# RWKV-7 scan and SwiGLU block in one kernel: gate and value matmuls all in half-height tiles, outputs in bursts on shared PSUM pairs

## The chip, the cores and the metric

The kernel runs on one core of a Trainium2 chip. A core has five engines that run their own instruction lists and wait for each other through semaphores: TensorE (PE, matmuls and transposes, with its weight loads shown apart as PEld), VectorE (DVE), ScalarE (ACT), GpSimd (POOL) and SyncE (SP), and beside them the DMA queues. PE writes its results to PSUM, here used as pairs of banks of 128 partitions x 2 x 512 numbers; DVE and ACT read them from there. Everything is computed in 32-bit floats.

The metric is the device time of one execution in microseconds. The profile is that of one execution; its span runs from the first to the last instruction.

## What is computed

A recurrent attention block (4 batches x 8 heads, 768 steps, head size 40) is followed by a gated feed-forward block on its output (3072 tokens x 320, inner size 1536). Cut to what matters:

```python
for t in range(S):                                   # S = 768
    y[:, :, t] = einsum('bhd,bhde->bhe', r_t, state)
    Sa = einsum('bhde,bhe->bhd', state, a_t)
    state = state * w_t[:, :, None, :] - einsum('bhd,bhe->bhde', Sa, b_t) \
            + einsum('bhd,bhe->bhde', v_t, k_t)
x = y.transpose(0, 2, 1, 3).reshape(B * S, H * D)    # 3072 x 320
xn = x / sqrt(mean(x * x, -1) + 1e-6) * rms_g
g, val = xn @ w_gate, xn @ w_val                     # 320 -> 1536, twice
out = (g * sigmoid(g) * val) @ w_out                 # 1536 -> 320
```

The three weight matrices arrive as 64-bit floats and are made into 32-bit ones on the chip.

## The kernel before

**The scan.** The 768 steps are cut into 24 chunks of 32 steps; one chunk of all batches is 128 tokens. For a chunk, `front(c)` loads r, k, v, w, a, b, turns them by PE transposes and builds products of decays over levels 1, 2, 4, 8, 16 and 32 (`gramk` matmuls on PE, many multiplications on DVE and copies on ACT). `inverse(c)` solves a small triangular system per head on DVE, with DMAs through DRAM before and after it. `main(c)` advances the state (`state`, `lower`, `update`), computes the outputs of the chunk (`score`, `level`, `y0`), turns them back (`turn4`), normalizes each token (ACT's square and scale, a power on POOL) and turns the result once more (`turn3`) into `xg`, the feed-forward's input with features on the partitions. The 320 features lie in `xg` as two blocks of 128 and one of 64, the last one twice, on the upper and on the lower 64 partitions. `front` and `inverse` of chunk c + 2 are created after `main(c)`.

**The feed-forward.** Chunks are gathered into groups by `GROUPS`: one chunk, eleven times two, one. After the last chunk of a group, `feed(g)` goes over the 1536 inner features in 12 slices of 128 (index `f`), two slices to a PSUM pair, a "room" (`plan.room()`). Gate lies in the first bank of the pair and value in the second. For a slice PE does the last 64 features first, gate on the upper 64 rows of the array beside value on the lower 64 (`h64`), then the two blocks of 128 features at full height, gate and then value (`hh`). ACT takes silu of the gate into `sg`, DVE multiplies value by it into `hT`, and PE multiplies `hT` by the slice's output weights (`out`) and adds that up over all 12 slices in `po`, a pair of its own that nothing else uses. After slice 12 ACT copies `po` to `o` and four DMAs write it out. Every matmul of 32-bit floats is two weight loads and two matmul instructions in the profile.

**The weights.** `narrow_slice(f)` loads the slices of the three weight matrices as raw 64-bit words and narrows them in two halves; each half is four DVE instructions and three of ACT, 24 halves in all. The slices are laid side by side in `wf[f]`. This is done during the first group; slices 2 to 11 are loaded through POOL's queue.

**The order.** Every step above is a "piece" for one engine (`plan.add`; `pe` puts several matmuls in one piece). All pieces are created first, with the pieces that each needs, and then issued in one order for all engines, written out by hand as 5993 numbers (`ORDER`): each is the place of a piece, counted from the first one not yet issued. An engine runs its pieces strictly in that order. The digits of `PAIRS` give each room one of three PSUM pairs; a pair is held from a room's first piece to its last. `plan.issue` also tells the framework where two instructions on one pair touch different banks or partition quarters and need not wait for each other.

All PE matmuls are issued through line 532 and transposes through line 535, DVE's instructions through line 486 (the narrowing's last one through 1050), ACT's through 509, 513, 516 and 1046, and DMAs through 529, so that the profile's rows are told apart by tiles: `ps<-xg,wf` is gate and value, `po<-wf,hT` the output.

Of the kernel before, what the change touches and what calls it, by code (L numbers as in the profile page):

```python
# [7 lines left out]
FP32 = mybir.dt.float32  # L8
I32 = mybir.dt.int32
# [11 lines left out]
GROUPS = (1,) + (2,) * 11 + (1,)  # L21
# [3 lines left out]
WARM = 230.0  # L25
# [380 lines left out]
def kernel(  # L406
# [587 lines left out]
    def feed(g):  # L994
# [5 lines left out]
        for f in range(LEAD if g == 0 else 0):  # L1000
            narrow_slice(f)
# [110 lines left out]
```

## Time and profile before

| what | before |
|---|---|
| runs, us | 1020.66, 1022.94, 1028.27 (median 1022.94) |
| span of the profiled execution, us | 1017.9 |
| median of the runs less that span, us | 5.0 |
| PE busy | 928.0 us, 91% |
| DVE busy | 779.5 us, 77% |
| ACT busy | 510.6 us, 50% |
| POOL busy | 343.2 us, 34% |
| mean granted TensorE clock | 0.953 of full |

How it is read: busy time is the union of an engine's instructions, and it is an average over stages; the page's slices show which engine is full when. A matmul's length in the profile holds the time until its result is out, so in a stream the distance between two starts is shorter than the length. The profile does not give the profiled execution's own time apart from its span; the median of the runs stands 5.0 us above it.

### The profile page before, as it was taken

The page shows a single profiled execution, that of the slowest core. Times are in us where ns is not written, and L with a number is a line of the kernel's source. Part 1 is how long each engine was busy: PE and PEld are TensorE (multiplying, and loading weights), DVE is VectorE, ACT ScalarE, POOL GpSimd, SP SyncE. Part 2 cuts the span into 40 slices and gives each one's busy share as a digit, 9 for nine tenths or more (in the row PEclk, how much of TensorE's full clock was granted, in tenths as well). Part 3 has the DMA queues.
Part 4 walks back from the last instruction along what each step waited for, and adds up shares of the span by engine and source line. Part 5 has one row for each costly group of instructions (what it writes and reads, how often), then busy time and mean ns, then how long its engine had stood idle before and what let it go on. Part 6 is the DMA issues. An engine that isn't in the chain of part 4 may idle for free.

```text
span 1017.9 us, 55372 instructions
## 1 busy us (share of the span) xinstructions
PE 928.0 (91%) x24512; PEld 754.3 (74%) x24512; DVE 779.5 (77%) x2718; ACT 510.6 (50%) x1134; POOL 343.2 (34%) x595
## 2 busy tenths in 40 slices
PE   3457779998999999999999999999999999999998
PEld 3446668877777777787877778777787787787776
DVE  9989987786967976967868779669688788776531
ACT  6878656544454544454463444544535545435131
POOL 9966543313233233224321433224233323400000
PEclk9657768999999999999999999999999999999999
DMA  7764543313333223233231242232322422420100
GB/s 170 159 178 109 124 91 78 74 32 69 52 67 63 51 60 75 43 67 68 48 75 32 61 88 48 50 70 45 70 58 46 78 48 60 76 45 9 45 6 20
DMA packets 140175, 68.87 MB, mean 68 GB/s; under 512 B 120768, under 2 KB 127264, under 8 KB 139936
## 3 DMA queue, kind: packets, MB, share of 16 engines
q0 software_dynamic: 19680, 32.48, 15.8%
q1 hardware_dynamic: 118080, 32.54, 15.2%
q8 instruction: 192, 3.15, 1.3%
q10 hardware_dynamic: 2176, 0.33, 0.2%
q14 instruction: 47, 0.39, 0.1%
HBM read 55.05 MB, written 10.22 MB: 64 GB/s over the span
## 4 chain that ended last, share of the span: by engine, by line
PE 71%; DVE 12%; issue 5%; DMA 5%; ACT 3%; SPq 3%; DVEq 0%; ACTq 0%
PE ps L532 50%; PE po L532 14%; PE ps L535 6%; SPq L529 3%; DVE Yi L486 3%; DMA sY<-Yi 2%; DVE tmp L486 2%; DVE As L486 1%; DVE y L486 1%; ACT VU L513 1%; DVE LT L486 1%; DMA sB<-LT 1%; DVE K L486 1%; DVE wf L486 1%; DMA LT<-sY 1%
## 5 line engine op out<-in xcount | busy, mean ns | idle before, releaser
L532 PE MATMUL ps<-xg,wf 128*128 128x256 f32 (+3 forms) x1872 | 360.5, 374 | 2.4 <-issue 1.6
L532 PEld LDWEIGHTS ps<-xg,wf 128*128 128x128 f32 (+1 forms) x1872 | 267.5, 189 | 50.6 <-issue 14.5
L532 PE MATMUL po<-wf,hT 128*128 128x320 f32 x576 | 180.5, 447 | 0.5 <-issue 0.5
L486 DVE TENSOR_TENSOR hT<-ps,sg 128x256 f32<-128x256 f32 (+1 forms) x156 | 59.9, 399 | 95.3 <-PE ps L532 53.7
L532 PEld LDWEIGHTS po<-wf,hT 128*128 128x128 f32 x576 | 102.6, 189 | 37.8 <-issue 3.7
L486 DVE TENSOR_TENSOR tmp<-Yi,M 128x24 f32<-128x24 f32 (+21 forms) x512 | 107.3, 210 | 12.2 <-DMA M<-sB 1.4
L486 DVE TENSOR_TENSOR Yi<-Yi,tmp 128x24 f32<-128x24 f32 (+21 forms) x512 | 107.1, 209 | 11.1
L509 ACT ACTIVATE sg<-ps 128x256 f32<-128x256 f32 (+1 forms) x156 | 54.1, 368 | 116.9 <-PE ps L532 114.1
L529 POOL DMA_DIRECT2D VU<-in_v_dram x92 | 54.1, 590 | 145.7 <-PE ps L532 145.6
L486 DVE TENSOR_TENSOR K<-K,T 128x256 f32<-128x256 f32 (+1 forms) x191 | 91.9, 496 | 2.1 <-ACT T L513 0.7
L529 POOL DMA_DIRECT2D kbn<-in_k_dram x92 | 53.9, 588 | 101.3 <-PE ps L532 98.3
L519 POOL TENSOR_TENSOR ss<-ss,mhalf 128x1 f32<-128x1 f32 x24 | 14.4, 599 | 214.7 <-DVE ss L486 214.6
L532 PE MATMUL ps<-Ab,K 64*60 64x56 f32 (+2 forms) x4608 | 77.9, 223 | 7.3 <-issue 2.2
L532 PEld LDWEIGHTS ps<-Ab,K 64*60 64x60 f32 (+2 forms) x4608 | 71.2, 135 | 17.0 <-issue 10.3
L513 ACT COPY KN<-ps 128x640 f32<-128x640 f32 x95 | 65.1, 691 | 33.4 <-DVE LT L486 22.4
L529 POOL DMA_DIRECT2D kbn<-in_b_dram x92 | 54.1, 589 | 77.5 <-PE ps L532 76.3
L486 DVE TENSOR_TENSOR As<-ps,msi 128x256 f32<-128x256 f32 (+1 forms) x168 | 70.5, 455 | 10.6 <-PE ps L532 6.4
L532 PEld LDWEIGHTS ps<-As,KN 128*40 128x40 f32 x3072 | 67.2, 128 | 12.9 <-issue 7.4
L532 PE MATMUL ps<-As,KN 128*40 128x32 f32 x3072 | 72.1, 208 | 4.2 <-issue 2.7
L513 ACT COPY K<-K 128x512 f32<-128x512 f32 x95 | 60.3, 635 | 23.5 <-PE ps L532 12.0
L486 DVE SCALAR_TENSOR_TENSOR Yi<-M,Yi 128x31 f32<-128x31 f32 (+6 forms) x228 | 44.7, 244 | 33.5 <-DMA M<-sB 17.1
L529 POOL DMA_DIRECT2D wn<-in_w_dram x92 | 52.1, 568 | 19.6 <-DVE KN L486 18.5
(138 smaller groups left out, 1525.4 us busy)
## 6 DMA issues: line engine op xcount, KB each, us to landing
M<-sB SPq DMA_DIRECT2D x96, 128.0 KB, 3.0
wan<-in_r_dram SPq DMA_DIRECT2D x24, 160.0 KB, 4.0
kbn<-in_b_dram POOLq DMA_DIRECT2D x92, 40.0 KB, 2.6
kbn<-in_k_dram POOLq DMA_DIRECT2D x92, 40.0 KB, 2.8
VU<-in_v_dram POOLq DMA_DIRECT2D x92, 40.0 KB, 2.8
wan<-in_a_dram POOLq DMA_DIRECT2D x46, 80.0 KB, 2.9
wan<-in_w_dram POOLq DMA_DIRECT2D x46, 80.0 KB, 3.0
wn<-in_w_dram POOLq DMA_DIRECT2D x92, 40.0 KB, 2.5
```

Source lines behind the costliest of these rows:

```text
L486: plan.add("DVE", time + more + each * size(o), 0.087, lambda at: [fn(at(o), *m(at))], [o], aps(*args))
L509: scalar(o, [a], lambda at: nc.scalar.activation(at(o), at(a), f, **kw), aps(acc), 0.1 if f in (AF.Square, AF.Relu) else 0.0)
L513: scalar(o, [a], lambda at: nc.scalar.copy(at(o), at(a)), extra=more)
L519: plan.add("POOL", 0.5, 0.06, lambda at: nc.gpsimd.tensor_tensor(o, a, b, op), [o], [a, b])
L529: plan.add(by, 0.6 if by == "POOL" else 0.45, 0.0, lambda at: queue.dma_start(out=o, in_=i), [o], [i], load=load, since=since)
L532: return o, lhsT, rhs, lambda at: nc.tensor.matmul(at(o), lhsT, rhs, start=start, stop=stop, skip_group_check=True), 4
L535: return o, i, ident, lambda at: nc.tensor.transpose(at(o), i, ident), 2
```

## The change

- Gate and value: the 320 features lie in `xg` as five blocks of 64, each twice, on the upper and the lower 64 partitions. All matmuls of gate use the upper 64 rows of the array, all of value the lower 64, five of each for a slice, issued in turn (two pieces: blocks 0 to 2, blocks 3 and 4). The weights are laid out for that, with three DMAs for each half of a slice (before two and four).
- To get `xg` in that form the normalized chunk is copied with each 64 features doubled, into the space of `As`; the normalized chunk itself takes the space of `y`. There are ten transposes and five scalings a chunk, before six and three.
- Silu writes `hT` directly and the multiplication works in place; `sg` is gone. `hT` is a ring: six tiles of two chunks, or twelve of one chunk, and three more wide ones in the narrowing's buffer `exs`.
- Outputs: `po` is gone. In a group of two chunks the outputs of six slices are issued as one run of pieces into a room taken for it; ACT copies the first such burst to `o`, DVE adds the second. In a group of one chunk all twelve slices make one burst.
- There are four PSUM pairs for all rooms, before three and `po`.
- `GROUPS` is four groups of one chunk, nine of two and two of one: 15 groups, before 13.
- `ORDER` has 6100 numbers and `PAIRS` 531 digits, all new. The unused warm-up matmul and a rule that bound a room's first piece to the needs of its later ones are gone.

```diff
-GROUPS = (1,) + (2,) * 11 + (1,)
+GROUPS = (1,) * 4 + (2,) * 9 + (1,) * 2
...
+HT = 6
...
-    WF = 5 * P + DM
-    GATE, VALUE, LAST = (0, P), (2 * P + DM, 3 * P + DM), (4 * P + DM,)
+    KP = DM // 64
+    WF = KP * P + DM
+    OUT0 = 3 * P
+    key_at = lambda j: slice(j * P, (j + 1) * P) if j < 3 else slice(j * P + DM, (j + 1) * P + DM)
...
-    plan = Plan([psum.tile([P, 2, 512], FP32, name=f"ps{i}") for i in range(3)],
+    plan = Plan([psum.tile([P, 2, 512], FP32, name=f"ps{i}") for i in range(4)],
...
-    sg_ = Turns(2, [P, 2, GT], "sg")
-    hT_ = Turns(2, [P, 2, GT], "hT")
+    hT_ = Turns(HT, [P, GT], "hT")
...
+    hH_ = Turns(0, [P, P], "hH")
+    hH_.tiles = [t[:, k * P:(k + 1) * P] for t in hT_.tiles for k in range(2)]
+    hT_.tiles += [exs[:, k * GT:(k + 1) * GT].bitcast(FP32) for k in range(3)]
...
-        copy(x[:, DM:], x[:, DM - 64:DM])
+        xd = As.rearrange("p j n i t -> p (j n i t)")[:, 0:KP * P].rearrange("p (k e) -> p k e", e=P)
+        copy(xd.rearrange("p k (d e) -> p k d e", d=2), x.rearrange("p (k e) -> p k e", e=64)[:, :, None].to_broadcast((P, KP, 2, 64)))
...
+        ps = plan.room()[:, :, 0:KP * 64].rearrange("p h (k t) -> p k h t", k=KP)
+        pe("turn3", [flip(ps[:, kt, h], xd[half(h), kt], ident[half(h), half(h)])
+                     for kt in range(KP) for h in range(2)])
...
+        ring = hT_ if W == GT else hH_
+        hTs, waiting = {}, []
+        step = FT if W < GT else FT // 2
+
+        def outs():
+
+            po = plan.room()
+            for f in waiting:
+                pe("out", [mm(po[:, q, 0:DM], hTs[f][:, q * P:(q + 1) * P], wf_[f][:, OUT0:OUT0 + DM], f == waiting[0], f == waiting[-1])
+                           for q in range(GROUPS[g])])
+            if waiting[0] == 0:
+                copy(o, po[:, 0:GROUPS[g], 0:DM])
+            else:
+                tt(o, po[:, 0:GROUPS[g], 0:DM], o, ADD)
+            waiting.clear()
...
-            pe("h64", [mm(h[e][:, q], wk[e][4][half(q)], x[half(q), 2, 0:W], e == 0, False) for e in range(2) for q in range(2)],
-               [hh])
             for e in range(2):
-                for q in range(2):
-                    pe("hh", [mm(h[e][:, q], wk[e][2 * q + kt], x[:, kt, 0:W], False, kt == 1) for kt in range(2)])
-                act(sgs[:, e, 0:W], h[e][:, 0], AF.Silu)
-                tt(hTs[:, e, 0:W], h[e][:, 1], sgs[:, e, 0:W], MUL)
-                pe("out", [mm(po[:, q, 0:DM], hTs[:, e, q * P:(q + 1) * P], wfs[e][:, 2 * P:2 * P + DM], f + e == 0, f + e == FT - 1)
-                                            for q in range(GROUPS[g])])
...
+                for part_ in (range(0, 3), range(3, KP)):
+                    pe("hh", [mm(h[e][:, q], wf_[f + e][half(q), key_at(kt)], x[half(q), kt, 0:W], e == 0 and kt == 0, kt == KP - 1)
+                              for kt in part_ for q in range(2)], [hh] if e == 0 and 0 in part_ else [])
+                hTs[f + e] = ring.next()
+                act(hTs[f + e][:, 0:W], h[e][:, 0], AF.Silu)
+                tt(hTs[f + e][:, 0:W], h[e][:, 1], hTs[f + e][:, 0:W], MUL)
+                waiting.append(f + e)
+            if len(waiting) == step:
+                outs()
```

More of the change, by code (lines that the diff above doesn't have):

```diff
@@ L258, with __init__ @@
 class Plan:
-    def __init__(self, pairs, stand_ins, warm_until):
+    def __init__(self, pairs, stand_ins):
         self.pieces, self.seen, self.masks = [], {}, {}
@@ L273, in room @@
         self.now[name] = len(self.rooms)
-        self.rooms.append([0, None, None])
+        self.rooms.append([0, None])
         return self.stand_ins[name]
@@ L332, in add @@
             room = self.rooms[piece.room]
-            room[2] = first = me if room[2] is None else room[2]
-            for i in needs:
-                if i < first and first not in self.pieces[i].users:
-                    self.pieces[i].users.append(first)
-                    self.pieces[first].missing += 1
             room[0] += 1
@@ L348, in issue @@
         for word in order.split():
-            if word == "-":
-                self.order.append(None)
-                self.warm()
-                continue
             i = first + int(word)
@@ L450 @@
     BH = B * H
-    KM = [min(P, DM - o) for o in range(0, DM, P)]
-    KT = len(KM)
     GT = CG * P
@@ L470, in side @@
         return t.rearrange("p n (g x l) -> p n g x l", x=2, l=l)[:, :, :, x, :]
-    plan = Plan([psum.tile([P, 2, 512], FP32, name=f"ps{i}") for i in range(3)],
-                [dram.tile([P, 2, 512], FP32, name=f"room{i}") for i in range(8)], WARM)
+    plan = Plan([psum.tile([P, 2, 512], FP32, name=f"ps{i}") for i in range(4)],
+                [dram.tile([P, 2, 512], FP32, name=f"room{i}") for i in range(8)])
     def size(ap):
@@ L556 @@
     select(ident, [[-1, P]], 0, 1)
-    po_ = psum.tile([P, 2, 512], FP32, name="po")
     nc.vector.memset(plan.pairs[0], 0.0)
@@ L561 @@
         nc.scalar.copy(t, plan.pairs[0])
-    nc.scalar.copy(po_[:, 0, DM:DM + P], plan.pairs[0][:, 0, 0:P])
     eye = const.tile([P, C // 4, C], FP32, name="eye")
@@ L593 @@
     nc.gpsimd.memset(c1792, -1792.0 * 128)
-    gcol = const.tile([P, KT], FP32, name="gcol")
-    for p0, kt, src in ((0, 0, 0), (0, 1, P), (0, 2, 2 * P), (64, 2, 2 * P)):
-        m = min(P, DM - src)
-        dma(gcol[p0:p0 + m, kt:kt + 1], moe_rms_g[src:src + m].rearrange("(d o) -> d o", o=1), "g", "POOL")
+    gcol = const.tile([P, KP], FP32, name="gcol")
+    for q in range(2):
+        dma(gcol[half(q)], moe_rms_g.rearrange("(j p) -> p j", p=64), "g", "POOL")
     blank(eye, 0.0)
@@ L977, in main @@
                      for m in range(4) for o in range(2)])
-        ss, x = ss_.next(), x_.next()
-        act(x[:, 0:DM].rearrange("p (m o e) -> p o m e", o=2, e=D), xv, AF.Square, acc=ss[:, 0:1])
+        ss, x = ss_.next(), y.rearrange("p n t -> p (n t)")[:, 0:DM]
+        act(x.rearrange("p (m o e) -> p o m e", o=2, e=D), xv, AF.Square, acc=ss[:, 0:1])
         ts(ss[:, 1:2], ss[:, 0:1], 1.0 / DM, EPS, MUL, ADD)
         ptt(ss[:, 2:3], ss[:, 1:2], mhalf, ALU.pow)
-        scale(x[:, 0:DM].rearrange("p (m o e) -> p o m e", o=2, e=D),
+        scale(x.rearrange("p (m o e) -> p o m e", o=2, e=D),
               xv, ss[:, 2:3])
-        copy(x[:, DM:], x[:, DM - 64:DM])
-        ps = plan.room()[:, :, 0:KT * 64].rearrange("p h (k t) -> p k h t", k=KT)
-        pe("turn3", [flip(ps[:, kt, h], x[half(h), kt * P:(kt + 1) * P], ident[half(h), half(h)]) for kt in range(KT) for h in range(2)])
+        xd = As.rearrange("p j n i t -> p (j n i t)")[:, 0:KP * P].rearrange("p (k e) -> p k e", e=P)
[3 more added lines that the diff above has]
+                     for kt in range(KP) for h in range(2)])
         g, at = group[c]
@@ L990, in main @@
             xg[g] = xg_.next()
-        for kt in range(KT):
+        for kt in range(KP):
             scale(xg[g][:, kt, at * P:(at + 1) * P].rearrange("p (h t) -> p h t", h=2), ps[:, kt], gcol[:, kt:kt + 1])
@@ L1001, in feed @@
             narrow_slice(f)
+        o = o_.next()[:, 0:GROUPS[g]]
+        ring = hT_ if W == GT else hH_
[11 more added lines that the diff above has]
+            waiting.clear()
         for f in range(0, FT, 2):
@@ L1034, in narrow @@
         rw = raw.rearrange("p (f w) -> p f w", w=2)[:, 0:n]
-        for to, src, load in srcs:
-            dma(to(rw).rearrange("p (k f) w -> p k f w", k=2) if load == "raw2" else to(rw),
-                src.bitcast(I32).rearrange("(k p) (f w) -> p k f w", k=2, w=2) if load == "raw2"
-                else src.bitcast(I32).rearrange("p (f w) -> p f w", w=2), load, "SP" if f < 2 else "POOL", since=S0 + S1 * f)
+        for to, src, load, k_ in srcs:
+            dma(to(rw).rearrange("p (k f) w -> p k f w", k=k_), src.bitcast(I32).rearrange("(k p) (f w) -> p k f w", k=k_, w=2),
+                load, "SP" if f < 2 else "POOL", since=S0 + S1 * f)
         lo, hi = rw[:, :, 0], rw[:, :, 1]
@@ L1051, in narrow @@
                  [dst], [low, ex])
[L1053 removed]
+    cut = WF // 2 - OUT0
     def narrow_slice(f):
         f0, f1 = f * P, (f + 1) * P
[L1057 to L1064 removed]
+        narrow(f, 0, wf_[f][:, 0:OUT0 + cut], [
+            (lambda t: t[half(0), 0:OUT0], moe_w_gate[0:192, f0:f1], "raw3", 3),
+            (lambda t: t[half(1), 0:OUT0], moe_w_val[0:192, f0:f1], "raw3", 3),
+            (lambda t: t[:, OUT0:], moe_w_out[f0:f1, 0:cut], "rawo", 1)])
+        narrow(f, 1, wf_[f][:, OUT0 + cut:], [
+            (lambda t: t[:, 0:DM - cut], moe_w_out[f0:f1, cut:], "rawp", 1),
+            (lambda t: t[half(0), DM - cut:], moe_w_gate[192:DM, f0:f1], "raw2", 2),
+            (lambda t: t[half(1), DM - cut:], moe_w_val[192:DM, f0:f1], "raw2", 2)])
     group = [(g, i) for g, m in enumerate(GROUPS) for i in range(m)]
@@ L1076 @@
             inverse(c + 2)
-    plan.warm = lambda: nc.tensor.matmul(po_[:, 0, DM:DM + P], ident, ident, start=False, stop=False, skip_group_check=True)
     plan.tc = tc
```

31 lines of the change are left out of this document (7 added, 24 removed), and 355 rows, old and new, of the table ORDER.

## The prediction, made before the changed kernel was run

> **What bounds the kernel now.** I read the page first: busy shares, slices, chain.
>
> ```profile
> span 1017.9 us, 55372 instructions
> ## 1 busy us (share of the span) xinstructions
> PE 928.0 (91%) x24512; PEld 754.3 (74%) x24512; DVE 779.5 (77%) x2718; ACT 510.6 (50%) x1134; POOL 343.2 (34%) x595
> ## 2 busy tenths in 40 slices
> PE   3457779998999999999999999999999999999998
> PEld 3446668877777777787877778777787787787776
> DVE  9989987786967976967868779669688788776531
> ...
> PE 71%; DVE 12%; issue 5%; DMA 5%; ACT 3%; SPq 3%; DVEq 0%; ACTq 0%
> ```
>
> There are two regimes. In the first seven or eight slices (25.4 us each) PE is half empty and VectorE (DVE) nearly full; from then on PE is full, and most of the chain that ended last is PE's. The view by stretches of time puts sizes to that.
>
> ```profile
> 0.00:200.00 200.00, 134.91 (x4842) 120.69 (x4842) 175.17 (x533) 137.07 (x274) 123.68 (x221) 0.76 0.55 124
> 200.00:950.00 750.00, 729.85 (x18965) 582.94 (x18953) 581.36 (x2101) 359.02 (x820) 218.95 (x373) 1.00 0.29 58
> ```
>
> Its columns are PE, weight loads, DVE, ACT, POOL, granted clock, DMA share, GB/s. Up to 200 us PE idles 65 us and DVE 25; from 200 to 950 PE idles 20.2 of 750 and DVE 169. So a saving counts in two places: feed work (gate, value, output) that PE can do before 200 us, and PE's own time after it. A busy PE is not yet a streaming PE, so next come PE's rows by shape, and two pieces of the timeline (start, length, what, how many).
>
> ```profile
> L532 PE MATMUL ps<-xg,wf 128*128 128x256 f32 x1056 | 258.4, 389 | 0.1
> L532 PE MATMUL po<-wf,hT 128*128 128x320 f32 x576 | 180.5, 447 | 0.5 <-issue 0.5
> L532 PE MATMUL ps<-xg,wf 64*128 64x256 f32 x528 | 72.7, 395 | 1.5 <-issue 1.0 <-DVE hT L486 0.3
> ...
> L532 PE MATMUL ps<-ST,aP 64*32 64x40 f32 x1472 | 18.2, 210 | 1.2 <-issue 1.2
> ```
>
> ```profile
> 965.87 6.64 PE L532 MATMUL ps<-xg,wf 128*128 128x256 f32 x30
> ```
>
> ```profile
> 964.16 1.46 PE L532 MATMUL ps<-xg,wf 64*128 64x256 f32 x12
> ```
>
> The length of a piece is its pitches plus the last matmul's own length. Full height: (6.64 - 0.389) / 29 = 0.216 us. Half height: the 12 are six pairs, gate on the upper rows beside value on the lower: (1.46 - 0.395) / 5 = 0.213 us a pair. **A pair of half-height matmuls streams in the time of one full-height one.** More of PE's timeline:
>
> ```profile
> 948.45 0.78 PE L532 MATMUL ps<-ST,aP 64*32 64x40 f32 x64
> 949.16 0.79 PE L532 MATMUL ps<-VU,LT 32*32 32x40 f32 x64
> ...
> 959.22 4.47 PE L532 MATMUL po<-wf,hT 128*128 128x320 f32 x16
> 963.62 9.10 PE L532 MATMUL ps<-xg,wf 64*128 64x256 f32 x48
> ...
> 988.24 2.42 PE L532 MATMUL po<-wf,hT 128*128 128x320 f32 x8
> 990.59 0.40 PE L535 MATMUL ps<-ident,x 64*128 64x64 f32 x6
> 990.92 1.34 PE L532 MATMUL po<-wf,hT 128*128 128x320 f32 x4
> 992.20 4.93 PE L532 MATMUL ps<-xg,wf 64*128 64x128 f32 x48
> 996.96 2.34 PE L532 MATMUL po<-wf,hT 128*128 128x320 f32 x8
> ```
>
> They price a **change of tile shape**. An output's pitch is (2.42 - 1.34) / 4 = 0.27 us, or 0.269 from the sixteen, (4.47 - 0.447) / 15. Eight outputs up to the next row's start take 2.35, which is 0.20 over 8 x 0.269, for entering and leaving. The sixteen take 4.40, 0.10 over, for leaving. The wide row of 48 is 16 half-height (8 pitches) and 32 full ones: 40 x 0.216 + 0.17 (the last one's length beyond its pitch) = 8.81, and 9.10 is 0.29 more, for its own start and the change inside it. One chunk wide, 48 take 4.76 to the next start; less 0.29, the 40 pitches are 0.112 each. Between two small shapes, the 64 of the state take 0.71 to the next start, at a pitch of (0.78 - 0.210) / 63 = 0.009, so 0.71 - 64 x 0.009 = 0.13 is the change. A change costs 0.13 to 0.20 us; I take 0.18, nearer the upper rows, because the changes that go are those beside wide matmuls.
>
> **The change part by part.** Counts of the new sequence come from its order list: each number is a place counted from the first piece not yet issued, and pieces stand as the functions create them.
>
> *Half-height gate and value, outputs in bursts.* The old list changes PE's shape 532 times, 180 of them into the full-height gates, values and outputs; the new one 415 times, 65 of them into outputs, now the only user of that shape. Nearly all of the difference lies past the start-up: 461 against 347 changes. 114 x 0.18 = **-20.5 us**; at the ends 114 x 0.13 = 15 and 114 x 0.20 = 23.
>
> *Streaming.* Before: 11 wide groups x 120 pitches x 0.216 and two narrow ones x 120 x 0.112, 312 us. After: nine wide and six narrow, 314 us. The matmuls of gate and value go from 1872 to 3600 instructions. Outputs stay 576 x 0.269. The transposes into xg go from 6 to 10 a chunk; six took 0.33 up to the next start, (0.33 - 0.13) / 6 = 0.03 each without the change, and 96 more are 3 us. Together **+5 us**.
>
> The Trainium skill, page "TensorEngine Tiling (Array Packing)", section Performance Considerations, speaks against this: it gives each matmul some 60 cycles of overhead, which for 1728 more matmuls I estimate at 43 us, so that the sum would be about 1033. The trace does not agree, since pairs at 0.213 carry twice the matmuls of 0.216; what remains of the rule is a rival below.
>
> *Smaller first groups, new order.* At 200 us, 533 DVE instructions had run, 11 of them multiplications of the feed. The two rows are the matmuls on xg and those on hT (with DVE third in the second):
>
> ```profile
> 0.00:200.00 200.00, 16.68 (x144) 14.93 (x144) 2.88 (x9) 0.76 0.55 124
> ```
>
> ```profile
> 0.00:200.00 200.00, 5.44 (x16) 2.64 (x16) 2.89 (x11) 0.76 0.55 124
> ```
>
> Up to that place, 522 DVE pieces of scan and weight conversion, the old list has 120 narrow and 12 wide pitches and 24 outputs, 22 us, beside 71 us of scan matmuls (each group's count by its pitch). Up to the same place the new list has 260 narrow pitches and 46 outputs, 41 us, beside 69. PE is 17 us ahead there. DVE, which sets that stretch, has done 14 more multiplications of 2.89 / 11 = 0.26 by then: +4. **-13 us.** PE's 65 idle us have room for it. The ends: 0, where that work delays the scan by what it wins, and -17.
>
> *Four pairs for all, outputs on one of them.* The old output pair lay idle between groups; now a burst holds a pair, and otherwise a fourth is free for all stages. What that can win past the start is PE's idle time with a named releaser:
>
> ```profile
> PE ps L532 <- issue: 23.3, 28, 2.3
> ...
> PE ps L535 <- DVE hT L486: 1.2, 2, 0.8
> ```
>
> Issue, the largest entry, has no releaser, and a pair does not cure it; the entries with one are small past the start. I take **-3 us**, nearest to these rows, with ends of -20 (all idle of the middle stretch) and +20 (twice as much).
>
> *What lies beside PE.*
>
> ```profile
> L513 ACT COPY KN<-ps 128x640 f32<-128x640 f32 x95 | 65.1, 691 | 33.4 <-DVE LT L486 22.4 <-PE ps L535 4.9 <-PE ps L532 4.1
> L513 ACT COPY K<-K 128x512 f32<-128x512 f32 x95 | 60.3, 635 | 23.5 <-PE ps L532 12.0 <-DVE K L486 3.7 <-DVE Yi L486 2.5
> L509 ACT ACTIVATE sg<-ps 128x256 f32<-128x256 f32 (+1 forms) x156 | 54.1, 368 | 116.9 <-PE ps L532 114.1 <-DVE tmp L486 2.5
> ```
>
> ```profile
> L486 DVE TENSOR_TENSOR hT<-ps,sg 128x256 f32<-128x256 f32 x132 | 53.6, 420 | 70.5 <-PE ps L532 46.6 <-ACT sg L509 19.8 <-ACT VU L513 3.5
> ...
> L486 DVE TENSOR_TENSOR ST<-ps,Sdec 128x640 f32<-128x640 f32 x22 | 18.1, 822 | 15.1 <-PE ps L532 11.3 <-ACT Yi L513 3.8
> ```
>
> A chunk now has ACT copy 640 columns instead of 64 and scale five blocks instead of three: at most 0.69 + 2 x 0.37 = 1.4 us in the chain from y to xg, 34 in all. DVE adds nine second bursts at 0.82 and 24 narrow multiplications, 14 us in all. Both hide under PE, which fills 730 of 750 us where ACT has 359 and DVE 581; with that cover gone the last chunk would show its 1.4 us. Silu now writes hT directly, and reuse of that ring waits for the burst that read it: nine wide tiles against six in a burst. Behind a waiting silu stand the scan's copies on ACT. Weight loads stay six DMAs a slice on SP and POOL; two small DMAs leave POOL and eight output DMAs join SP, which only issues.
>
> **Sum.** 1017.9 - 20.5 + 5 - 13 - 3 = 986.4 of span. The median of the runs, 1022.94, lies 5.0 above the span, which I carry over: 991, rounded to **990 us**, 3.2% faster.
>
> **The rivals.**
>
> *The lead is eaten.* Gate matmuls placed early in PE's fixed order stand ahead of scan matmuls that DVE waits for, and the start-up grows by what it won: 990 + 13 = 1003. For it: at a clock of 0.76 each such piece is longer. Against: DVE has the next chunks' work to go on with.
>
> *Four pairs win more.* All 20 us of idle go: 990 - 17 = 973.
>
> *The added matmuls cost their start.* The tightest pitch in the rows is the state's 0.009: 1728 x 0.009 = 16, so 1006. The page named above would have it so, and worse.
>
> *Slower: a room's tail becomes PE's wait.* Gate and value of a slice now end together, so silu (0.37) and multiplication (0.42) both follow the last matmul: 0.79 us. There are 15 x 6 = 90 rooms of two slices each; in the new list 44 have a matmul of the second slice behind the first one's silu, which reads the same bank. If PE stands 0.79 in all 90, that is 71 us: 1061. It turns the sign from 42 of them (33 / 0.79). Against: the old list has 38 such of 78, and PE's row for hT shows 1.2 us.
>
> *It doesn't do what it says:* pairs that take turns over long runs would add 314 us, 1304. The measured pair speaks against it.
>
> **How the numbers follow.** Chances: forecast 0.53 (its own range 976 to 1004, from the ends of the change's price and half of those of the idle time), lead eaten 0.14, four pairs 0.14, start cost 0.05, slower 0.12 and no pairs 0.02. For 8 in 10 the range takes in the forecast, the eaten lead, the start cost and most of the fourth pair: 962 to 1016. One per cent, 10 us, is about what this kernel's measurement can tell. Faster: 0.53 + 0.13 + 0.14 + 0.04 less 0.03 for tails, 0.81; slower: the room's tail without its mildest cases and no pairs, 0.13; the rest 0.06.
>
> **What would show it.** Right: half-height rows at 0.21 us a pair throughout; some 500 matmuls on xg and 40 on hT by 200 us, where 144 and 16 stood; PE's idle time in the middle stretch under 25 us; fewer and longer output rows. Wrong: PE waiting on hT or silu by tens of us, DVE idle well past 25 us before 200, PE's unnamed idle well past 23 us, or pairs at twice their pitch.

## The result, and the profile after

The changed kernel takes 1060.68 us (median of four runs, 1053.63 to 1072.08) where the kernel before takes 1022.49 on the same chip: a ratio of 1.0343, 95% interval 1.0296 to 1.0391. The forecast was 990, the range 962 to 1016. Ratios here and below leave out executions that fell in the chip's slower state (here the one of 1072.08), so that they differ a little from the quotient of the medians. The profiled execution took 1059.3 us. From the page of after (the changed kernel): the span, the busy shares, and two engines in 40 slices of 26.4 us.

```profile
span 1057.5 us, 59054 instructions
...
PE 932.3 (88%) x26336; PEld 778.8 (74%) x26336; DVE 776.3 (73%) x2751; ACT 537.4 (51%) x1208; POOL 345.8 (33%) x593
...
PE   4466789899899998999999998999888999899998
...
DVE  8887985866768787787687787797696697786431
```

PE's busy time is up by 4 us only; its span is up by 40. It isn't slower at its work, it stands more: the 9s of the middle slices now have 8s among them. The view by stretches (PE, weight loads, DVE, ACT, POOL, clock, DMA share, GB/s), and under it the first stretch for the matmuls on xg alone:

```profile
0.00:200.00 200.00, 135.85 (x4706) 121.06 (x4706) 161.95 (x506) 135.00 (x275) 119.38 (x215) 0.83 0.53 118
200.00:950.00 750.00, 696.45 (x19730) 574.07 (x19734) 573.27 (x2105) 371.56 (x851) 224.79 (x376) 0.98 0.28 57
```

```profile
0.00:200.00 200.00, 31.76 (x452) 28.54 (x452) 5.13 (x15) 0.83 0.53 118
```

By 200 us PE has run 452 matmuls on xg where it had run 144 (a slice takes 1.92 times as many now, so 452 are the work of 235 old ones). But DVE, which sets that stretch, is at 506 instructions where it was at 533, and 20 of the 506 are the feed's multiplications where 11 were. In the middle PE idles 54 us of 750 where it idled 20, and DVE gets no further for it. Who PE and DVE wait for, over the whole span (us, times, longest), after and, for DVE, before. Line numbers differ from kernel to kernel; in after, PE's matmuls are L473 and its transposes L476, DVE's line is L427, and ACT's are L450, L454 and L457:

```profile
PE ps L473 <- DVE hT L427: 15.2, 16, 3.3
PE ps L473 <- issue: 13.6, 15, 1.8
PE ps L473 <- DVE K L427: 12.5, 6, 9.4
PE ps L476 <- DVE y L427: 6.8, 7, 3.5
```

```profile
DVE hT L427 <- ACT hT L450: 80.6, 40, 10.1
DVE LT L427 <- ACT KN L454: 29.0, 21, 4.3
...
DVE hT L427 <- PE ps L473: 14.7, 10, 2.8
```

```profile
DVE hT L486 <- PE ps L532: 53.7, 29, 8.3
DVE hT L486 <- ACT sg L509: 33.8, 17, 6.8
```

The multiplication used to wait mostly for matmuls, 54 us, which is how it should be when PE is the bound; now it waits for the silu on ACT, 81 us, and PE waits for the multiplication.

**An account of PE.** I took every matmul's start-to-start gap, from all of PE's records: up to the pitch of its shape it is streaming; where the shape changes, the next 0.18 us is change; an excess of over 0.12 us elsewhere, or beyond the change, is a wait; the small rest stands with the changes. First to last matmul, in us:

| | streaming | changes + small rest | waits | waits up to 200, 200 to 950, later |
|---|---|---|---|---|
| before | 796 | 66 + 34 | 108 | 68, 39, 1 |
| after | 798 | 58 + 2 | 188 | 73, 107, 8 |

By this account changes and small overheads fell by 40 us, and the waits took 80. The sum, 40 us more, is sure; the split hangs on the line between a small rest and a wait. With every shape's median pitch, and the two matmuls of a pair taken together, the same records give waits of 94 and 144. The profile's own measure, PE's idle time with a named releaser in the middle stretch, goes from 5 to 45 us.

For the middle stretch I also set each wait of PE beside the last thing that released it, by the list's own needs and by a rule that both traces show without an exception: of two instructions on different engines that touch the same bank and quadrant (32 partitions) of a pair, the later in the list starts only when the earlier has ended, even for other columns. Before: 8 us for a pair handed over from another room, 0.5 for a reader in the same room, 9 for data. After: 40, 16 and 28. The Trainium skill, page "PSUM — Partial Sum Buffer", section "PSUM bank collisions raise a hardware error", has this rule (a dependency by bank and quadrant, reads too, not by address); the traces agree. A stretch of the timeline of after shows what the rule does (start, length, what, idle time before):

```profile
511.61 0.38 ACT L450 ACTIVATE hT<-ps 128x256 f32<-128x256 f32 x1 [2.04 <-PE ps L473]
...
515.29 1.54 PE L473 MATMUL ps<-xg,wf 64*128 64x256 f32 x12
...
516.88 0.76 DVE L427 TENSOR_TENSOR hT<-ps,hT 128x256 f32<-128x256 f32 x2 [1.29 <-PE ps L473]
...
517.36 1.14 PE L473 MATMUL ps<-xg,wf 64*128 64x256 f32 x8 [0.22 <-DVE hT L427]
```

The room's first slice has its silu done at 512.0, yet its multiplication starts at 516.88, behind the first twelve matmuls of the second slice, which write the same two banks; and the other eight of the second slice start when that multiplication ends, at 517.30.

### The profile page after: what moved, and what is told of

It reads as the page before. It is cut to its first block, busy times and chain, and to the rows that moved or that the text cites. A ratio compares the mean times of both kernels' runs of the same rounds, so it can differ in the third digit from the quotient of the medians.

```text
span 1057.5 us, 59054 instructions
## 1 busy us (share of the span) xinstructions
PE 932.3 (88%) x26336; PEld 778.8 (74%) x26336; DVE 776.3 (73%) x2751; ACT 537.4 (51%) x1208; POOL 345.8 (33%) x593
## 5 line engine op out<-in xcount | busy, mean ns | idle before, releaser
L473 PE MATMUL ps<-xg,wf 64*128 64x256 f32 (+1 forms) x3600 | 369.4, 351 | 19.0 <-DVE hT L427 10.5
L473 PEld LDWEIGHTS ps<-xg,wf 64*128 64x128 f32 x3600 | 294.7, 194 | 52.0 <-DVE hT L427 13.0
L473 PE MATMUL ps<-wf,hT 128*128 128x320 f32 x432 | 130.7, 445 | 1.8 <-ACT xg L457 0.9
L427 DVE TENSOR_TENSOR tmp<-Yi,M 128x24 f32<-128x24 f32 (+21 forms) x512 | 106.6, 208 | 17.6 <-DMA M<-sB 7.1
L427 DVE TENSOR_TENSOR hT<-ps,hT 128x128 f32<-128x128 f32 (+1 forms) x144 | 48.5, 353 | 95.4 <-ACT hT L450 80.6
L427 DVE TENSOR_TENSOR Yi<-Yi,tmp 128x24 f32<-128x24 f32 (+21 forms) x512 | 106.6, 208 | 9.7
L473 PE MATMUL ps<-Ab,K 64*60 64x56 f32 (+2 forms) x4608 | 81.3, 224 | 25.1 <-DVE K L427 12.5
L473 PEld LDWEIGHTS ps<-wf,hT 128*128 128x128 f32 x432 | 77.8, 189 | 31.5 <-DVE hT L427 1.1
L473 PEld LDWEIGHTS ps<-Ab,K 64*60 64x60 f32 (+2 forms) x4608 | 73.3, 136 | 36.6 <-issue 10.8
L427 DVE TENSOR_TENSOR K<-K,T 128x256 f32<-128x256 f32 (+1 forms) x191 | 91.5, 495 | 3.0 <-ACT K L454 1.1
L450 ACT ACTIVATE hT<-ps 128x128 f32<-128x128 f32 (+1 forms) x144 | 45.2, 332 | 92.9 <-PE ps L473 92.4
L454 ACT COPY KN<-ps 128x640 f32<-128x640 f32 x95 | 65.0, 694 | 35.4 <-PE ps L473 15.2
L427 DVE TENSOR_TENSOR As<-ps,msi 128x256 f32<-128x256 f32 (+1 forms) x168 | 74.7, 457 | 10.9 <-ACT As L457 6.3
L473 PE MATMUL ps<-As,KN 128*40 128x32 f32 x3072 | 70.4, 204 | 9.2 <-ACT As L457 4.3
L473 PEld LDWEIGHTS ps<-As,KN 128*40 128x40 f32 x3072 | 64.7, 124 | 18.3 <-ACT As L457 5.5
L460 POOL TENSOR_TENSOR ss<-ss,mhalf 128x1 f32<-128x1 f32 x24 | 19.8, 825 | 155.3 <-DVE ss L427 154.4
L454 ACT COPY K<-K 128x512 f32<-128x512 f32 x95 | 60.5, 637 | 12.2 <-DVE K L427 5.6
L427 DVE SCALAR_TENSOR_TENSOR Yi<-M,Yi 128x31 f32<-128x31 f32 (+5 forms) x228 | 43.6, 244 | 28.8 <-DMA M<-sB 20.5
```

Source lines behind the costliest of these rows:

```text
L427: plan.add("DVE", time + more + each * size(o), 0.087, lambda at: [fn(at(o), *m(at))], [o], aps(*args))
L450: scalar(o, [a], lambda at: nc.scalar.activation(at(o), at(a), f, **kw), aps(acc), 0.1 if f in (AF.Square, AF.Relu) else 0.0)
L454: scalar(o, [a], lambda at: nc.scalar.copy(at(o), at(a)), extra=more)
L460: plan.add("POOL", 0.5, 0.06, lambda at: nc.gpsimd.tensor_tensor(o, a, b, op), [o], [a, b])
L473: return o, lhsT, rhs, lambda at: nc.tensor.matmul(at(o), lhsT, rhs, start=start, stop=stop, skip_group_check=True), 4
```

## The experiments

Ratios are to the kernel before on the same chip, with 95% intervals. "Searched list" means: single numbers of `ORDER` and `PAIRS` were moved by a program that replays the list (each instruction starts when its engine is free and what it waits for has ended, with durations and pitches from the traces) and keeps what shortens the replay. "Counted" means that the replay also makes two instructions on one bank of a room follow the order of the list. On the traced lists the replay gives after 1022 us with the order in shared banks inside a room and 987 without it, and before 1020 with it and less than 1 less without.

**Only the threading.** Every engine's own order stays, only how the five are threaded into one list is new.

```diff
 ORDER = """
-(after's numbers)
+(the same sequence for each engine, threaded anew)
```

> The changed kernel with the order on every engine exactly as it was; only how the engines' orders are threaded into one list differs, and with it which of two instructions in a bank waits for the other. Theory: 10 to 20 us come back, 1040 to 1050, since about a third of the bank waits can be turned round without reordering an engine. Rivals (slow parts; an engine's own order is unlucky): within 5 us of the changed kernel, 1056 to 1066.

1064.42 us, 1.0302 [1.0240, 1.0365]: nothing won that can be told from the change, as the rivals had it. This other threading doesn't help; it is one of many, so that the loss lies in each engine's own order is likely and not shown.

**A first search, three lists.** After's instructions, with the banks of a room counted and not, and before's instructions.

```diff
 ORDER, PAIRS = (a searched list)
```

> The changed kernel's instructions, all of them and no others, in another written order (and other pairs for the rooms). The order was searched for with the durations that the traces show, counting that two instructions of different engines in one bank of a room run in the order of the list. Theory (waits inside a bank, set by the list): PE's idle time from 200 to 950 us falls from 54 to under 20 us, and the time to 975 to 1000 us. Rival (the new parts are slow themselves: the tail of silu and multiplication, ACT's added copies, four pairs): no list helps by more than 20 us, 1040 or more. Rival (merely an unlucky list): 975 to 1000 as well; the next run parts it from the theory.

> As the run before, from the same starting list with the same search, except that the search counts waits inside a room only where one instruction reads what another wrote, not where they merely share a bank. Theory: the waits in the banks come back, some 50 to 60 us of PE's time past 200 us, 1030 to 1060. Rival (merely an unlucky list): as fast as the run before, 975 to 1000. Rival (slow parts): 1040 or more, like the run before.

> The kernel before with its own instructions and a list from the same search (banks counted): what the search is worth by itself. Theory: the old list has hardly any wait in a bank (PE's idle time past 200 us with a named releaser is a few us), so only some 24 shape changes (4 us) and some of the start-up go, 1000 to 1015. If the search alone were worth what the first run shows, it would be 950 to 965, and the first run would say nothing on the change.

1126.0 us, 1.0913 [1.0840, 1.0986]; 1151.55, 1.1171 [1.1119, 1.1223]; 1119.86, 1.0887 [1.0821, 1.0953]. A miss: the lists are bad for both kernels, by some 60 and 90 us. The replay lacked a cost: on DVE an instruction that needs the result of the one right ahead of it starts 0.034 us after that one's end, any other 0.084 us before it, and the search had put 943, 937 and 914 such neighbours side by side, where before has 865 and after 759. At 0.118 us each that is up to 22 us for after's instructions and 6 for before's, so most of the miss has another cause, which I didn't find. What survives is the pair of which only one counted the banks: 25 us lie between them.

**The second search**, with those 0.118 us and later landings of the DMAs: after's instructions with the banks counted, before's instructions likewise (the edit takes out of before the rule that bound a room's first piece, which the change had dropped), and after's with the banks of a room not counted.

```diff
 ORDER, PAIRS = (a searched list)
 # before's instructions only:
-            for i in needs:
-                if i < first and first not in self.pieces[i].users:
-                    self.pieces[i].users.append(first)
-                    self.pieces[first].missing += 1
```

> The changed kernel's instructions in a list from a second search. The first search had overlooked what the runs since showed: on VectorE an instruction that needs the result of the one right ahead of it starts 0.034 us after that one's end, any other 0.084 us before it, 0.118 us for each of 759 to 943 such places in the lists run so far. This search counts it, later DMA landings, and the waits in a bank. Theory (the parts are sound, their list is not): 980 to 1010, with PE's idle time from 200 to 950 us under 30 us. Rival (the parts are slow themselves): no list of theirs comes under 1030.

> The kernel before with its own instructions in a list from the same second search: what searching is worth by itself. Expected: 1000 to 1020, since PE has 20 us of idle time past 200 us to give and the shape changes stay near 520. If it falls by as much as the changed kernel does with its new list, the search and not the parts made the difference there.

> The counterpart of the run with the new list (ratio 1.004 to before): the changed kernel's instructions, the same start, the same second search, as long, but counting a wait inside a room only where one instruction reads what another wrote, not where two engines merely share a bank. Theory (a room's two slices share banks, and which waits for which is set by the list): the bank waits come back, 40 to 70 us over the other list, a ratio of 1.04 to 1.07. Rival (the list matters, the banks don't): within 10 us of the other list, 0.995 to 1.015.

1033.84 us, 1.0039 [1.0003, 1.0076]; 1059.01, 1.0287 [1.0235, 1.0338]; 1091.0, 1.0611 [1.0540, 1.0683]. So another list alone brings the change's instructions from 1.034 to 1.004, and two lists of which only one counted the order in shared banks lie 57 us apart (one list each, so part of it may be luck of the search). The first two missed what I expected, by 24 and 39 us: 1033.84 is no gain over before, and the rival of slow parts, no list under 1030, still stands. Before's instructions lost 2.9% to their own hand-made list, so the search itself costs; at equal search the change's parts beat before's by 25 us. The middle stretch of the first, and under it that of the last:

```profile
200.00:950.00 750.00, 706.01 (x19928) 586.04 (x19926) 570.44 (x2121) 372.91 (x854) 222.16 (x376) 0.99 0.30 59
```

```profile
200.00:950.00 750.00, 677.97 (x19034) 559.62 (x19032) 546.95 (x2025) 353.00 (x811) 220.09 (x373) 0.98 0.28 56
```

PE idles 44 us in the one and 72 in the other.

**The room's tail, in the kernel before.** Its own list; only gate and value of a slice now end together, as in the change. 111 of 5993 places had to move back.

```diff
-                for q in range(2):
-                    pe("hh", [mm(h[e][:, q], wk[e][2 * q + kt], x[:, kt, 0:W], False, kt == 1) for kt in range(2)])
+                for kt in range(2):
+                    pe("hh", [mm(h[e][:, q], wk[e][2 * q + kt], x[:, kt, 0:W], False, kt == 1) for q in range(2)])
```

> The kernel before with one thing taken over from the change: gate and value of a slice end together. Its full-height matmuls go kt 0 of gate and value, then kt 1 of both, in place of the whole gate and then the whole value; the same matmuls, the same shapes, the old list with 111 of 5993 places moved back because silu now needs both pieces. Theory (the tail of a room stands in PE's way): PE waits for silu and multiplication 20 to 60 us more, 1035 to 1075. Rival (the tail is covered by other rooms' work): within 10 us of before, 1013 to 1033.

1076.01 us, 1.0451 [1.0412, 1.0489]. PE's waits there:

```profile
PE ps L530 <- DVE hT L484: 17.2, 17, 2.9
...
PE ps L530 <- ACT sg L507: 7.1, 14, 1.1
```

Before, PE waited 1.5 us for hT, in two rows, and had no row for the silu. In the old order the gate's bank is done two matmuls ahead of the value's, so a reader works in one bank while PE writes the other; with both open to the end, a list made for that alternation loses 47 us (the 111 places moved back are in this number; they weren't tried alone). PE's waits for a reader of the same room go from 0.5 to 24 us in the middle stretch, for pairs handed over from 8 to 15, for data from 9 to 20.

**The silu left out**, in both kernels.

```diff
-                act(hTs[f + e][:, 0:W], h[e][:, 0], AF.Silu)
-                tt(hTs[f + e][:, 0:W], h[e][:, 1], hTs[f + e][:, 0:W], MUL)
+                tt(hTs[f + e][:, 0:W], h[e][:, 1], x[:, 0, 0:W], MUL)
```

> The changed kernel with its own list and its silu left out: the multiplication takes the value times a block of xg from SBUF, so that hT is not the reference's. The tail behind a slice's last matmul is the multiplication alone, 0.42 us in place of 0.79. Theory (the tail is on PE's path): 15 to 40 us less than the changed kernel's 1061, 1020 to 1046. Rival (it is covered): within 8 us, 1052 to 1068.

> The kernel before with its own list and its silu left out in the same way. Here the value's two full-height matmuls, 0.43 us, run between the gate's last one and the multiplication, so silu's 0.37 us lie beside them. Theory: within 8 us of before, 1014 to 1032. If it gains as much as the changed kernel does, the gain is ACT's relief and not the tail.

1059.69 us, 1.0296 [1.0230, 1.0362], and 1030.8, 1.0010 [0.9973, 1.0046]. A tail shorter by a whole instruction is worth about 5 us, within the uncertainty of nothing, as the rival had it. The length of the tail is not the price.

**The feed's readers taken out of the banks.** First for the first slice of each room, then for both; list and pairs untouched (the same edits in before, with `sgs`).

```diff
-                act(hTs[f + e][:, 0:W], h[e][:, 0], AF.Silu)
-                tt(hTs[f + e][:, 0:W], h[e][:, 1], hTs[f + e][:, 0:W], MUL)
+                act(hTs[f + e][:, 0:W], h[e][:, 0] if e else x[:, 0, 0:W], AF.Silu)
+                tt(hTs[f + e][:, 0:W], h[e][:, 1] if e else x[:, 1, 0:W], hTs[f + e][:, 0:W], MUL)
```

> The change with its own list and pairs; the silu and the multiplication of the first slice of each room read blocks of xg in SBUF instead of the room's gate and value banks, so that this slice's result is left out of the computation and nothing but matmuls touches a bank while the second slice is written. Theory (shared banks in the feed's rooms are a good part of the loss): replaying the list without these readers gives 14 us less, so 1046 us, a ratio of 1.015 to 1.025 instead of 1.034. Rival (the feed's rooms are not it): within 4 us of the change, 1.030 or more.

> The same edit in the kernel before, with its own list: the first slice's silu and multiplication read SBUF, so that this slice's result is left out. There the two banks alternate, and the replay gives 1 us less. Theory and rival alike: a ratio of 0.995 to 1.0. If it gains as much as the changed kernel does, the gain is not that of the shared banks but of a reader that waits for nothing.

> As in fs_after, but silu and multiplication of both slices of every room read SBUF, so that the results of gate and value are left out and no reader of the feed holds a bank pair; list and pairs are the change's own. Theory of the handover (pairs that the feed's readers release late are a good part of the loss): the trace of the change has 17 us of PE's waits at pairs handed over by a reader of the feed and 10 at readers of the same room, of which fs_after took 5; if PE's waits are worth what they last, some 15 us more go, 1040 us, a ratio of 1.01 to 1.02. Rival (other waits take their place, as the replay of the list has it: 4 us more): 1.023 to 1.03.

> The same edit in the kernel before, with its own list, so that the results of gate and value are left out: 8 us of handover in its middle stretch, 2 us less by the replay. A ratio of 0.993 to 1.001 by theory and rival alike.

1060.12 us, 1.0292 [1.0251, 1.0333]; 1031.34, 1.0011 [0.9979, 1.0043]; 1057.0, 1.0215 [1.0139, 1.0291]; 1032.9, 1.0023 [0.9994, 1.0052]. Readers of the first slices cost the change some 5 us (PE's waits for a reader of the same room fall from 16 to 8), within the uncertainty of nothing and nearer to the rival than to the theory. All readers of the feed cost some 13, by the difference of two ratios whose intervals leave 4 to 22. This number is weak: of five executions one took 1042 us and four 1054 to 1059, and the four alone would give 7. The ratio lies between theory and rival. The replay had 14 for the first step and 4 more for the second, so its first step was wrong. Two thirds of the loss or more stay with the feed's rooms as good as free. In that run PE still waits 30 us for pairs handed over and 40 for data; that this lies in the order of the scan's pieces, in the same list, is what remains, and no run shows it.

**A longer search**, against several sets of disturbed durations: after's instructions, before's, and after's with a pair kept for the outputs and three for all else.

```diff
 ORDER, PAIRS = (a searched list)
```

> The change's instructions, a list and pairs from the same longer search that gave before's instructions 1.0147 of the time before. Theory (the new instructions cost PE less, and the loss of the change lies in waits that its list made): the lead of some 2.4% over before's instructions at equal search holds, so a ratio of 0.98 to 1.0, 1003 to 1024 us, against 1.034 with its own list. Rival (the parts are worth nothing, the list is all): 1.010 to 1.02, like before's instructions.

> The same longer search over the instructions of before. Theory: as with the search before it, the parts of the change keep a lead of about 25 us at equal search, so 1015 to 1045 us, a ratio of 0.99 to 1.02, and 2 to 3% above the changed kernel's instructions under the same search. Rival (the parts are worth nothing, the list is all): the two within 1% of each other.

> The change's shapes, groups and bursts, but outputs keep a pair of their own as before and all other rooms share three; list and pairs from the same search as g1b_third (1.0058), which has left it with 498 changes of shape against some 430. If four shared pairs are worth something at equal search: 15 to 25 us above that run, a ratio of 1.02 to 1.03. If it is their sharing that makes the waits: at most that run's ratio, 1.006. The search had not settled here, so that a small difference upward decides nothing.

1034.83 us, 1.0058 [1.0027, 1.0088]; 1040.21, 1.0147 [1.0092, 1.0201]; 1043.2, 1.0145 [1.0100, 1.0191]. A first list of this search for after's instructions, of which I had expected 995 to 1020 us, gave no time. The change's parts lead again, by 9 us (3 to 15) instead of 25, less than I expected; sharing four pairs is worth 9 us or nothing (that search had not settled). No list that I found brings the change below the kernel before.

That asked for a reason: in the longer search's run of after's instructions PE's waits with a releaser are down to 15 us in the middle stretch (before: 17), and its shapes are the cheaper ones. From the list of PE's waits over its whole span:

```profile
PE ps L518 <- issue: 47.4, 52, 2.8
```

Issue, for which the profile names no releaser, had 23.3 us before. **These stalls sit at fixed places of PE's count.** Numbered from PE's first matmul, the long gaps inside runs of one shape lie whole multiples of 127.3 apart: in before 31 of 38 fall into 8 of every 127.3 places. The queue that brings instructions moves blocks of about as many: 24512 matmuls with their weight loads came in 192 packets of 16 KB, 127.7 to each. Its row (packets, MB, share) of before:

```profile
q8 instruction: 192, 3.15, 1.3%
```

**A last run was to move the count, not the work**: 64 small matmuls more, early, where PE idles.

```diff
 ORDER = """
 ...
+- - - (64 times, behind PE's third piece)
 ...
-    plan.warm = lambda: nc.tensor.matmul(po_[:, 0, DM:DM + P], ident, ident, start=False, stop=False, skip_group_check=True)
+    plan.warm = lambda: nc.tensor.matmul(po_[0:32, 0, 0:32], ident[0:32, 0:32], ident[0:32, 0:32], start=True, stop=True, skip_group_check=True)
```

> The kernel before with 64 small matmuls more on PE in the start-up, behind its third piece, where PE idles; their result isn't read. All later matmuls stand 64 places further on in PE's count. If the stalls without a releaser inside runs of one shape come from the supply of instructions in blocks of 128 matmuls, their places in the new count lie again in the first half of each 128 (four in five of some 20 to 30) and they fall on other matmuls. If they come from the work itself, they fall on the same matmuls, now in the second half. The time stays within 1% either way.

1038.15 us, 1.0090 [1.0059, 1.0121]. This run does not part the two. Each of the 64 matmuls is two matmul instructions in the profile (24640, where before has 24512), so the count moved by 128, a whole block, and every later matmul kept its place in its block. Of the 19 unnamed stalls over 0.3 us inside runs of one shape in its middle stretch, 18 fall on a matmul that stalled before, and both readings would have that. One of them, the same matmul in before and in this run:

```profile
234.90 0.64 PE L532 MATMUL ps<-VU,KN 64*40 64x40 f32 x47
237.24 0.38 PE L532 MATMUL ps<-VU,KN 64*40 64x40 f32 x17 [1.70 <-issue]
```

```profile
253.18 0.64 PE L531 MATMUL ps<-VU,KN 64*40 64x40 f32 x47
255.49 0.38 PE L531 MATMUL ps<-VU,KN 64*40 64x40 f32 x17 [1.67 <-issue]
```

**What parts them are the other traces.** The searched lists bring other matmuls to these places, and the stalls stay at the places: in all 20 traces together, all 662 unnamed stalls of that kind past the first 127 matmuls lie between the 85th and the 113th of every 127.3 matmuls. And they end when instructions have come: in 656 of the 662, PE goes on 1.15 to 1.7 us after a packet of that queue has landed, a distance at which only one matmul in ten starts otherwise. So at these places PE stands for its instructions.

What stalls at these boundaries cost, and what else PE waits, in the middle stretch (us, from the same records):

| | before | after | second search, after's | longer search, after's | longer search, before's |
|---|---|---|---|---|---|
| at block boundaries | 21 | 11 | 36 | 44 | 31 |
| all other waits | 18 | 96 | 50 | 38 | 23 |

A list that takes PE's other waits away runs into its instruction supply. After has 26336 matmul instructions where before has 24512, and half-height ones use a block up in half the time (128 x 0.108 = 14 us instead of 28). The Trainium skill, page "Runtime: NRT & Kernel Launch", section "Instruction fetch mechanics", has the blocks (16 KiB, 256 instructions), which the count bears out. It calls the crossing mostly hidden: inside runs of one shape 32 of before's blocks stall for over 0.3 us and 53 of the longer search's, of some 200 each, and all boundary stalls together are 35 and 62 us, which is not nothing. The run with 64 matmuls more is 0.9% slower although its boundary stalls are no longer in sum (36 us): the stall shown comes 18 us later than in before, of 22 us between the two spans, so most was lost by then. Why, I can't say.

## Why the prediction was wrong, point by point

- **Half-height gate and value, bursts: -20.5.** Right in its mechanism, perhaps too small: 415 changes as counted, pairs stream at 0.216 us throughout, and changes and small overheads fell by up to 40 us. 117 fewer changes at my price are 21 of them; what the others are isn't settled.

- **Streaming: +5.** Measured +2.

- **Smaller first groups: -13.** The lead came (452 matmuls on xg by 200 us where I had some 500) and was eaten, as the first rival had it: DVE is 27 instructions behind at that place, 36 without the feed's multiplications, at 750 / 2105 us each 10 to 13 us; and PE's waits up to 200 us are 73 where they were 68.

- **Four pairs for all: -3, ends -20 and +20.** This is the step that failed. It read what the pairs could win from the idle time of the old list and took the new list to be as tight. PE's waits grew by 68 us in the middle stretch and 7 at the end, where my outer end was 20: 32 for pairs handed over, 15 for readers of the same room, 19 for data, of the part that has a releaser. Even the profile's plain idle time with a releaser grew by 40 there. That the list carries most of the loss is shown by the runs that change the list alone (1.034 to 1.004; 57 us between two lists); that the order in shared banks can cost as much, by the two pairs of lists that differ in counting it (25 and 57 us). Which share of the loss it has in the change's own list is not settled: the replay says 35 us but falls some 36 short of after's span (1022 for 1057.5), the feed's readers account for 7 to 13 on the chip, and the scan's rooms could not be tried without changing what the scan computes.

- **What lies beside PE.** The work of ACT and DVE did hide, but not its place: DVE waits 81 us for the silu where I had costed the ring and the burst alone.

- **The slower rival named the number, 1061, and the first half of its mechanism.** Gate and value that end together do cost 47 us in before, with its old list. But its price, 0.79 us in each of 90 rooms, is not what is paid, so that the number fits is luck: without the silu 5 us come back. What is paid, as far as the waits show, are the readers' places in the list against the matmuls of the next slice and of the next room. My point against it, that the old list has 38 such places and PE hardly waits there, missed that in the old kernel the reader's bank and the bank being written alternate.

- **The added matmuls cost their start.** Not as I priced it (the pitch holds), but 1824 more matmul instructions bring 14 more blocks; at equal search, boundary stalls are 10 to 20 us longer over the span with the change's parts. That is one reason why the lead that they keep is small.

- **Signs.** PE's idle time past 25 us in the middle (54), PE waiting on hT or silu (21 us with the tiles in exs, before 1.5) and DVE's idle time before 200 us (38 against 25) were named as what would show the forecast wrong, and did. PE's unnamed idle and the pairs' pitch, the two others, stayed in bounds.

## What to carry to other kernels

An idle time in the old profile bounds what a new buffer can win, not what a new order can lose: where a change brings its own order, count for it each reader that stands between two writers of its PSUM bank, before its instructions are priced. Two instructions that alternate between banks hide a reader for nothing; making both banks end together gives that up, and shortening the reader did not bring it back here. And when PE's named waits are gone, look at its unnamed ones by their place in its count of instructions: fewer instructions may then be worth more than cheaper ones, which no run here has tried.

## What the runs showed of the hardware

- PE stalls at some boundaries of its instruction blocks (127.3 matmuls with their weight loads), most by 0.3 to 2.5 us, some 20 to 60 us a kernel, and goes on 1.15 to 1.7 us after a packet of the queue that brings instructions has landed.
- On DVE an instruction that needs the result of the one right ahead starts 0.034 us after that one's end, an independent one 0.084 us before it.
- A pause of PE of 1.1 to 3.3 us can be followed by 3.4 or 6.8 us at half clock. It need not be: past 200 us, before pauses for 1.70 and 1.67 us and after for 1.69 us at full clock. From the view by stretches of after, behind the pauses that end at 231.7 and 273.6 us (the clock is the third column from the end):

```profile
232.00:235.40 3.40, 3.40 (x38) 3.40 (x38) 2.95 (x16) 0.00 (x0) 0.00 (x0) 0.51 0.00 0
235.40:256.00 20.60, 18.36 (x618) 15.54 (x618) 18.01 (x51) 10.73 (x27) 9.07 (x16) 1.00 0.25 49
...
273.50:280.30 6.80, 6.71 (x122) 6.49 (x122) 4.56 (x23) 1.86 (x6) 0.00 (x0) 0.55 0.01 4
280.30:297.00 16.70, 15.65 (x454) 13.28 (x444) 13.79 (x47) 6.17 (x16) 5.78 (x10) 1.00 0.23 46
```

Five such stretches past 200 us, 24 us together, bring the mean of the middle to 0.98, where before has 1.00. I estimate their cost at up to 12 us, half their length, which the account above has partly in its waits and partly in its small rest. So a wait on PE can cost more than it lasts.
